# A Fourier mixing layer with a leaky-ReLU MLP: VectorE's work put in the program's own order, with the preparation of the next unit at fixed steps

## The chip, the cores and the metric

The kernel runs on one core of one Trainium2 chip. The time is the device time of one execution in microseconds (us); times given as "the runs" are medians over several executions, and the profile is one further execution, recorded by the hardware profiler. The core has five engines with a queue each: PE (TensorE, the matrix multiplier, whose weight loads are listed apart as PEld), DVE (VectorE), ACT (ScalarE), POOL (GpSimd) and SP (SyncE, which here issues transfers). Each engine works through its own queue in order, and semaphores tie the queues together.

## What is computed

```python
X = np.fft.fft(x, axis=1)            # x: (8, 3008, 256) float32
X = np.fft.fft(X, axis=2)
attn_out = X.real.astype(np.float32)

x = attn_out.reshape(8 * 3008, 256)
h = x @ w_in                          # w_in: (256, 2048)
g = np.maximum(0.01 * h, h)
return (g @ w_out).astype(np.float32) # w_out: (2048, 256)
```

The transform over the 256 features is folded into `w_in` once, at the start; the transform over the 3008 rows is made per batch by folding the rows with additions and subtractions (VectorE) and multiplying the folded rows with small tables of cosines and sines (TensorE).

## The kernel before

**Units, chunks, steps.** Each of the 8 batches is cut into two units by the parity `c` of the output frequency: `units = [(b, c) for b in range(B) for c in (1, 0)]`, so unit number `n` is even for `c = 1` and odd for `c = 0`. A unit has three chunks ("parts" 0, 1, 2) of 250 or 251 columns, and a chunk has 8 steps `f = 0..7`, each of which takes one pair of the 16 blocks of the hidden layer. From chunk 2 on, a step is written (part, f) below; the same (part, f) comes back in every unit, some 16 times in the run.

**What one step does** (`step`, L922). `up` (L818) multiplies a chunk's transformed rows with the folded `w_in` into two PSUM tiles, `cos_ps` and `sin_ps`, by 4 listed matmuls each. `activate` puts them together on VectorE: two scalar_tensor_tensor (L827), one add (L831), one subtract (L832); ScalarE applies the leaky ReLU (L833); GpSimd makes four sums and differences of the result (L840 to L843). `down(at - 3)` multiplies what the step three back made with `w_out` (L891, 14 listed matmuls) into four PSUM tiles `sum_ps`, where all 8 steps of a chunk add up. After a chunk's last step, ScalarE copies one sum (L900), VectorE makes 7 additions out of the four tiles (L915), and SP stores the result. Because of the lag of three steps, those 7 additions stand in step f = 2 of the following chunk. `sum_ps` has four buffers in all, so the first `down` of the following chunk (in step f = 3) writes over the tiles that the 7 additions read. `cos_ps`, `sin_ps` and the transform's `dft_ps` share four other PSUM buffers.

**What is prepared beside it for the next unit.** In an odd unit, `fold_x` folds the rows of the next batch, in eight items: 0 and 2 add the mirrored rows of the first and second half (L327), 1 and 3 fold its columns (L334 and L336), 4 to 7 fold the two halves into each other (L343, one each). `xs[b + 1] = load_x(b + 1)` issues the four transfers of that batch from SP's queue in step (2, 6) of the even unit before; the tile `xt` has one buffer. In every unit but the first and last, `fold_rows` folds the rows further for each of the two feature halves (its `part` 0 and 1) of the next unit: `fold_even` and `fold_odd`, with `turn` (L363 and L364 on ScalarE, L366 and L367 on VectorE) and adds (L393, L394, L402, L403, L406 to L410). `dft` then makes the 16 transform matmuls (L633) and a butterfly of additions on VectorE (L661 to L733), which ends in the tile `mix` that the next unit's `up` reads.

**Who sets the order.** The program is built by a scheduler that orders each engine's queue by its own estimate of when an instruction can start; inside `with tc.manual_schedule(engines={...})` the named engines keep the order in which the program issues their instructions. Before, VectorE has the program's order up to step 34 (the step (1, 2) of unit 1), and from step 35 on the scheduler's. TensorE, ScalarE, GpSimd and SP are ordered by the scheduler from step 16 on, before and after.

Of the kernel before, what the change touches and what calls it, by code (L numbers as in the profile page):

```python
# [271 lines left out]
def tile_fnet_leaky_relu(  # L272
# [35 lines left out]
    def load_x(b):  # L308
        t = x_tile()
        for h in range(2):  # L310
            for odd in range(2):
                load_rows(t, b, h, odd)
        return t
# [10 lines left out]
    def add_mirrors(t, h, rows):  # L324

        a, z = t[:, h, 0, rows], t[:, h, 1, rows]
        nc.vector.tensor_tensor(a, a, z, op=ALU.add)  # L327

    def fold_columns(t, h, part, rows):


        a, z = t[:, h, 0, rows], t[:, h, 1, rows]
        if part == 0:
            nc.vector.tensor_tensor(z[:, :, 0:P], a[:, :, 0:P], a[:, :, P:D], op=ALU.add)  # L334
        else:
            nc.vector.tensor_tensor(z[:, :, P + 1 : D], a[:, :, 1:P], a[:, :, P + 1 : D], op=ALU.subtract)  # L336

    def fold_halves(t, part, c, rows, to=None):

        i, cols = (c + part) % 2, slice(part * P, (part + 1) * P)  # L340
        z = t[:, :, 1, rows, cols]
        to = t[:, i, 0, rows, cols] if to is None else to[:, rows]
        nc.vector.tensor_tensor(to, z[:, 0], z[:, 1], op=(ALU.add, ALU.subtract)[i])  # L343

    def fold_x(b, at):

        t, rows = xs[b], slice(0, NT)
        h, i = divmod(at, 2)
        if h < 2 and i == 0:
            add_mirrors(t, h, rows)  # L350
        elif h < 2:
            for part in range(2):
                fold_columns(t, h, part, rows)
        else:
            fold_halves(t, i, 3 - h, rows)
        if at == 7:
            zs[b] = xs.pop(b)
# [56 lines left out]
    def rows_of_x(b, part, c):  # L414

        t = zs[b]
        src = t[:, (c + part) % 2, 0, :, part * P : (part + 1) * P]
        return Rows(src, [t[:, part, 1].rearrange("p c (i d) -> p (c i) d", i=2)], part, c)

    class Direct:  # L420
# [5 lines left out]
        def even_rows(self, m):  # L426

            pe, n = dft_ps(), (KW[self.c] + 1) // 2
            for i, (chunk, to) in enumerate(((1, pe[0:m, 0 : 2 * n]), (0, pe[0:m, 0:n]), (2, pe[0:m, n : 2 * n]))):
                at, rows = (i + 1) * n if i else 0, slice(0, FROWS if i else P)  # L430
                nc.tensor.matmul(to, lhsT=self.src[rows, chunk], rhs=self.tab[0][rows, at : at + to.shape[1]],  # L431
                                 start=(i == 0), stop=(i == 2), skip_group_check=True)
            return pe

        def odd_rows(self, m, lo=0, hi=KW[1]):

            po, n = dft_ps() if m == P else sum_ps(), KW[1]
            for i in range(FI):
                rows = slice(0, FROWS if i < 2 else P)
                nc.tensor.matmul(po[0:m, 0 : hi - lo], lhsT=self.src[rows, FI + i],  # L440
                                 rhs=self.tab[1 + i // 2][rows, i % 2 * n + lo : i % 2 * n + hi], start=(i == 0), stop=(i == 2))
            return po
# [20 lines left out]

    rows_of = {}

    def fold_rows(u, part):
        rows = rows_of[u, part] = rows_of_x(u[0], part, u[1])
        rows.fold_even()
        rows.fold_odd()


    feat_sb = const.tile([P, 2, 2 * P], F32, name="feat_sb")
# [264 lines left out]
    def mix(u, blk, direct=False):  # L737

        t = work.tile([P, UW[0]], F32, tag=f"mix{blk}", bufs=2, name=f"mix{blk}")
        mixed.setdefault(u, {})[blk] = t  # L740
        return butterfly(t, P, blk, u[1], direct=direct)

    def dft(u, blk):
        rows = rows_of.pop((u, blk))
        banks = even_rows(rows, P), odd_rows(rows, P)
        for made, bank in zip(mix(u, blk), banks):
            made(bank)

    def dft_direct(part):

        rows, made = evens[part], mix(units[1], part, direct=True)
        made[0](rows.even_rows(P))
        po = rows.odd_rows_even(P)
        made[1](po)
        made[2](po)
# [16 lines left out]
    def spread(u):  # L772

        b, c = u
        t = work.tile([P, UW[0]], F32, tag="nb", bufs=2, name="nb")
        nc.sync.dma_start(t[:, 0 : UW[c]], nyq_dram[b, c, 0 : UW[c]].partition_broadcast(P))
        spreads[u] = t
# [18 lines left out]
    units = [(b, c) for b in range(B) for c in PARITIES]  # L796
    blocks, _ = chunks()
    plain = 2
    steps = [(j, f) for f in range(NH) for j in range(plain)]
# [6 lines left out]
    def up(j, f):  # L806
        raised(j, f)
        activate(j, f)
# [108 lines left out]

    lag = 3

    folds = {(0, 1): (0,), (0, 3): (1,), (0, 4): (2,), (0, 5): (3,), (0, 6): (4, 5), (0, 7): (6,), (1, 0): (7,)}  # L920
    first_folds = {(0, 1): (0,), (0, 3): (1,), (0, 4): (2,), (0, 5): (3,), (0, 6): (4,), (0, 7): (5,), (1, 0): (6,), (1, 1): (7,)}

    def step(at):
        if at < len(steps):
            j, f = steps[at]
            up(j, f)
            n, part = divmod(j, 3)
            b, c = units[n]
            if n == 0 and f == 4:
                dft_direct(1)  # L930
            if 0 < n < len(units) - 1:
                if part == 0 and f == 4:
                    spread(units[n + 1])
                at_steps = folds if n > 1 else first_folds
                if n % 2 == 1 and (part, f) in at_steps:
                    for i in at_steps[part, f]:
                        fold_x(b + 1, i)
                if part > 0 and f == 3:
                    fold_rows(units[n + 1], part - 1)
                if part > 0 and f == 5:  # L940
                    dft(units[n + 1], part - 1)
            if n % 2 == 0 and part == 2 and f == 6 and b + 1 < B:
                xs[b + 1] = load_x(b + 1)
        if at - lag >= done:
            down(*steps[at - lag])
# [10 lines left out]
    with tc.manual_schedule(engines={mybir.EngineType.DVE, mybir.EngineType.PE, mybir.EngineType.SP}):  # L956
        with tc.manual_schedule(engines={mybir.EngineType.Pool, mybir.EngineType.Activation}):
# [56 lines left out]
            u, first, others = units[0], (0, CW), (CW, KW[1])  # L1014
# [21 lines left out]
            odd = [direct.odd_rows(P, *first) for direct in (cosine, sine)]  # L1036
# [6 lines left out]
            odd = [direct.odd_rows(P, *others) for direct in (cosine, sine)]  # L1043
# [78 lines left out]
    for at in range(16, 23):  # L1122
        step(at)

    with tc.manual_schedule(engines={mybir.EngineType.DVE}):
        for at in range(23, 35):
            step(at)
    for at in range(35, len(steps) + lag):
        step(at)


# [35 lines left out]
```

## Time and profile before

| what | value |
|---|---|
| median of 4 runs | 1900.11 us (1899.07 to 1901.16) |
| the profiled execution, its own time | 1899.83 us |
| span of its instructions | 1898.0 us |
| granted TensorE clock over the span | 0.999 |
| DVE, L827 (two in a step) | 470 ns each |
| DVE, L831 and L832 | 676 and 669 ns |
| ACT, L833 | 1040 ns |
| POOL, L840 to L843 | 756, 863, 674, 743 ns |
| DVE, L327 / L334 / L336 / L343 (folds of x) | 2139 / 1232 / 1079 / 1288 ns |
| DVE, L366 / L367 (turns) | 617 / 549 ns |
| DVE, L915 (a chunk's last additions) | 408 to 415 ns |
| ACT, L363 / L364 (for the turns) | 391 / 386 ns |

The span is the time from the first to the last instruction that the profiler recorded; the execution's own time is 1.83 us longer. Times inside the trace are counted from the span's start. A row of the trace gives a start, a duration, an engine and a line; a bracket behind it tells how long the engine had been idle and what ended the idle time. Listed durations of neighbouring matmuls overlap, because they are pipelined: what a matmul takes in the stream is the distance between starts, 0.21 us for 250 or 251 columns.

### The profile page before, as it was taken

Reading aid. Unit: us, or ns where it says so; the run is one execution under the profiler, and the core shown is the slowest. Engines: PE = TensorE matmul, PEld = TensorE weight load, DVE = VectorE, ACT = ScalarE, POOL = GpSimd, SP = SyncE. Lnnn points to the kernel's source line nnn. Section 1 sums busy time; section 2 is a strip of 40 time slices with the busy share of each in tenths; the row PEclk is TensorE's granted clock in tenths of the full one; section 3 lists DMA queues with packets and bytes.
Section 4 is the critical chain, followed back from the end, with each engine's and each line's share of the span. In section 5 each row is a group of like instructions: output and inputs, shape, how many; then the busy total and the mean of one; then the engine's idle time right before and its main releaser. Section 6 shows DMA issues by size and latency. Waiting matters only on the chain.

```text
span 1898.0 us, 25260 instructions
## 1 busy us (share of the span) xinstructions
PE 1890.6 (100%) x9088; PEld 1679.7 (89%) x9088; DVE 1275.0 (67%) x2543; ACT 500.8 (26%) x674; POOL 1103.9 (58%) x1510
## 2 busy tenths in 40 slices
PE   9999999999999999999999999999999999999999
PEld 7888888988889888898888988888888888888987
DVE  8857865696656965569555796558865588555554
ACT  3522322232222322223222232222322223222222
POOL 1236555576555765558555675556655566555554
PEclk9999999999999999999999999999999999999999
DMA  7311000110002000020000200002000020000000
GB/s 252 114 62 78 12 20 23 46 74 12 31 11 100 20 22 20 12 108 16 18 20 12 108 22 12 20 12 110 21 12 19 16 115 12 20 12 22 12 12 23
DMA packets 34349, 78.74 MB, mean 41 GB/s; under 512 B 5536, under 2 KB 20000, under 8 KB 34224
## 3 DMA queue, kind: packets, MB, share of 16 engines
q1 hardware_dynamic: 33792, 76.86, 11.0%
q8 instruction: 73, 1.20, 0.3%
q14 instruction: 52, 0.43, 0.1%
q10 hardware_dynamic: 432, 0.26, 0.0%
HBM read 52.40 MB, written 24.71 MB: 41 GB/s over the span
## 4 chain that ended last, share of the span: by engine, by line
PE 98%; DVE 1%; DMA 0%; issue 0%; ACT 0%; DVEq 0%
PE sum_ps L891 58%; PE cos_ps L818 17%; PE sin_ps L818 17%; PE sum_ps L871 3%; PE dft_ps L633 3%; PE wf_ps L577 1%; DMA raw<-in_w_in_dram 0%; DVE xt L327 0%; PE dft_ps L431 0%; DVE xt L334 0%; DVE xt L336 0%; DVE power L542 0%; DVE win L543 0%; DVE power L525 0%; PE dft_ps L458 0%
## 5 line engine op out<-in xcount | busy, mean ns | idle before, releaser
L833 ACT ACTIVATE g<-g 128x1004 f32<-128x1004 f32 (+1 forms) x384 | 399.2, 1040 | 1126.0 <-DVE g L832 1059.5
L827 DVE SCALAR_TENSOR_TENSOR cos<-nb,wn,cos_ps 128x251 f32<-128x251 f32 (+1 forms) x768 | 330.2, 470 | 525.4 <-PE cos_ps L818 523.0
L840 POOL TENSOR_TENSOR s<-g 128x251 f32<-128x251 f32 (+1 forms) x368 | 278.2, 756 | 666.2 <-ACT g L833 660.3
L891 PE MATMUL sum_ps<-s,wt 128*128 128x251 f32 (+1 forms) x2208 | 528.4, 374 | 0.0
L891 PEld LDWEIGHTS sum_ps<-s,wt 128*128 128x128 f32 x2208 | 414.9, 188 | 55.0 <-POOL s L841 1.8
L818 PE MATMUL cos_ps<-mix,wf 128*128 128x251 f32 (+1 forms) x1536 | 387.9, 374 | 0.0
L818 PE MATMUL sin_ps<-mix,wf 128*128 128x251 f32 (+1 forms) x1536 | 387.8, 374 | 0.0
L891 PE MATMUL sum_ps<-g,wo 128*128 128x251 f32 (+1 forms) x1472 | 373.0, 375 | 0.8 <-DVE o L915 0.8
L818 PEld LDWEIGHTS cos_ps<-mix,wf 128*128 128x128 f32 x1536 | 291.2, 190 | 34.2 <-ACT power L526 0.5
L818 PEld LDWEIGHTS sin_ps<-mix,wf 128*128 128x128 f32 x1536 | 290.3, 189 | 34.8
L841 POOL TENSOR_TENSOR s<-s,g 128x251 f32<-128x251 f32 (+1 forms) x368 | 317.7, 863 | 0.0
L891 PEld LDWEIGHTS sum_ps<-g,wo 128*128 128x128 f32 x1472 | 277.0, 190 | 33.0 <-DVE o L915 1.2
L843 POOL TENSOR_TENSOR s<-g,s 128x251 f32<-128x251 f32 (+1 forms) x368 | 273.5, 743 | 28.9
L831 DVE TENSOR_TENSOR g<-cos,sin_ps 128x502 f32<-128x502 f32 (+1 forms) x384 | 259.4, 676 | 43.8 <-DVE cos L827 6.9
L832 DVE TENSOR_TENSOR g<-cos,sin_ps 128x502 f32<-128x502 f32 (+1 forms) x384 | 257.0, 669 | 0.0
L842 POOL TENSOR_TENSOR s<-g 128x251 f32<-128x251 f32 (+1 forms) x368 | 248.2, 674 | 0.0
L891 PE MATMUL sum_ps<-s,wo 128*128 128x251 f32 (+1 forms) x736 | 215.8, 375 | 0.0
L891 PE MATMUL sum_ps<-g,wt 128*128 128x251 f32 (+1 forms) x736 | 215.8, 375 | 0.0
L891 PEld LDWEIGHTS sum_ps<-s,wo 128*128 128x128 f32 x736 | 139.5, 190 | 16.3
L891 PEld LDWEIGHTS sum_ps<-g,wt 128*128 128x128 f32 x736 | 139.8, 190 | 15.8
L915 DVE TENSOR_TENSOR o<-e,sum_ps 128x251 f32<-128x251 f32 (+1 forms) x180 | 66.0, 408 | 0.0
L871 PE MATMUL sum_ps<-g,wo 128*128 128x251 f32 x256 | 57.1, 374 | 0.5 <-DVE wo L543 0.5
(130 smaller groups left out, 825.7 us busy)
## 6 DMA issues: line engine op xcount, KB each, us to landing
xt<-in_x_dram SPq DMA_DIRECT2D x28, 1024.0 KB, 7.6
out_dram<-o SPq DMA_DIRECT2D x78, 251.0 KB, 2.3
raw<-in_w_in_dram SPq DMA_DIRECT2D x8, 512.0 KB, 6.2
raw<-in_w_out_dram SPq DMA_DIRECT2D x8, 512.0 KB, 4.6
out_dram<-o SPq DMA_DIRECT2D x16, 250.0 KB, 2.1
xt<-in_first_x_dram SPq DMA_DIRECT2D x4, 768.0 KB, 8.8
nb<-nyq_dram SPq DMA_DIRECT2D x8, 376.5 KB, 3.4
nb<-nyq_dram SPq DMA_DIRECT2D x7, 376.0 KB, 3.5
```

The lines of the kernel that those rows point to most:

```text
L818: nc.tensor.matmul(pt[blk][:, h * n : (h + 1) * n], lhsT=wf[:, blk, fs[h] * P : (fs[h] + 1) * P], rhs=mixed[b, c][blk][:, at : at + n], st ...
L827: nc.vector.scalar_tensor_tensor(cos[:, hs], in0=spreads[b, c][:, at : at + n], scalar=wn[:, fs[h] : fs[h] + 1], in1=pt[0][:, hs], op0=ALU ...
L831: nc.vector.tensor_tensor(g[:, 0], cos[:, 0 : 2 * n], pt[1][:, 0 : 2 * n], op=ALU.add)
L832: nc.vector.tensor_tensor(g[:, 1], cos[:, 0 : 2 * n], pt[1][:, 0 : 2 * n], op=ALU.subtract)
L833: nc.scalar.activation(g, g, ACT.Lrelu)
L840: nc.gpsimd.tensor_tensor(s1, a[1][0], a[1][1], op=ALU.add)
L841: nc.gpsimd.tensor_tensor(s2, s1, a[0][0], op=ALU.subtract)
L842: nc.gpsimd.tensor_tensor(s3, a[0][0], a[1][0], op=ALU.subtract)
L843: nc.gpsimd.tensor_tensor(s4, a[0][1], s2, op=ALU.subtract)
L871: nc.tensor.matmul(sums[j][d][:, r * n : (r + 1) * n], lhsT=wo[:, fs[h] // NH, fs[h] % NH, d * P : (d + 1) * P], rhs=a[r][h], start=(f == ...
L891: nc.tensor.matmul(sums[j][p], lhsT=still[p], rhs=moving[p], start=(f == 0 and i % 2 == 0), stop=(f == NH - 1), skip_group_check=True)
L915: nc.vector.tensor_tensor(to, x, y, op=ALU.add)
```

## The change

Three things. From step 35 to the end VectorE keeps the program's order, as it did for steps 23 to 34. The eight items of `fold_x` get one list of places for all batches, one item a step, with none at f = 1 or 2 of part 0 (there were two lists, one for the first odd unit and one for the others, and the second put two items in one step). `fold_rows` is split into its even and its odd half, which are issued in successive steps, and the transform of the first feature half is issued two steps later.

| issued in step (part, f) | before, unit 1 | before, later units | after |
|---|---|---|---|
| x items 0 to 7 (odd units) | (0,1) (0,3) (0,4) (0,5) (0,6) (0,7) (1,0) (1,1) | (0,1) (0,3) (0,4) (0,5) (0,6) twice (0,7) (1,0) | (0,3) (0,4) (0,5) (0,6) (0,7) (1,0) (1,1) (1,3) |
| rows, half 0, even / odd | (1,3) / (1,3) | (1,3) / (1,3) | (1,4) / (1,5) |
| transform, half 0 | (1,5) | (1,5) | (1,7) |
| rows, half 1, even / odd | (2,3) / (2,3) | (2,3) / (2,3) | (2,3) / (2,4) |
| transform, half 1 | (2,5) | (2,5) | (2,5) |

```diff
-    def fold_rows(u, part):
-        rows = rows_of[u, part] = rows_of_x(u[0], part, u[1])
-        rows.fold_even()
-        rows.fold_odd()
+    def fold_rows(u, part, odd):
+        if not odd:
+            rows_of[u, part] = rows_of_x(u[0], part, u[1])
+            rows_of[u, part].fold_even()
+        else:
+            rows_of[u, part].fold_odd()
...
-    folds = {(0, 1): (0,), (0, 3): (1,), (0, 4): (2,), (0, 5): (3,), (0, 6): (4, 5), (0, 7): (6,), (1, 0): (7,)}
-    first_folds = {(0, 1): (0,), (0, 3): (1,), (0, 4): (2,), (0, 5): (3,), (0, 6): (4,), (0, 7): (5,), (1, 0): (6,), (1, 1): (7,)}
+    folds = {(0, 3): 0, (0, 4): 1, (0, 5): 2, (0, 6): 3, (0, 7): 4, (1, 0): 5, (1, 1): 6, (1, 3): 7}
+
+    row_folds = {(1, 4): (0, 0), (1, 5): (0, 1), (2, 3): (1, 0), (2, 4): (1, 1)}
+    transforms = {(1, 7): 0, (2, 5): 1}
...
-                at_steps = folds if n > 1 else first_folds
-                if n % 2 == 1 and (part, f) in at_steps:
-                    for i in at_steps[part, f]:
-                        fold_x(b + 1, i)
-                if part > 0 and f == 3:
-                    fold_rows(units[n + 1], part - 1)
-                if part > 0 and f == 5:
-                    dft(units[n + 1], part - 1)
+                if n % 2 == 1 and (part, f) in folds:
+                    fold_x(b + 1, folds[part, f])
+                if (part, f) in row_folds:
+                    fold_rows(units[n + 1], *row_folds[part, f])
+                if (part, f) in transforms:
+                    dft(units[n + 1], transforms[part, f])
...
     with tc.manual_schedule(engines={mybir.EngineType.DVE}):
-        for at in range(23, 35):
+        for at in range(23, len(steps) + lag):
             step(at)
-    for at in range(35, len(steps) + lag):
-        step(at)
```

## The prediction, made before the changed kernel was run

> **What bounds the kernel now.** I read the page's shares and its chain first, then the waits of TensorE, then the timeline around each wait.
>
> ```profile
> PE 1890.6 (100%) x9088; PEld 1679.7 (89%) x9088; DVE 1275.0 (67%) x2543; ACT 500.8 (26%) x674; POOL 1103.9 (58%) x1510
> ...
> PE 98%; DVE 1%; DMA 0%; issue 0%; ACT 0%; DVEq 0%
> ```
>
> TensorE is busy from end to end and is 98% of the chain. The change neither adds nor removes a matmul, so it can only win back moments in which TensorE waits, or make new ones. Its waits from step 23 on, out of the list of waits (us in total, times, longest):
>
> ```profile
> PEld sum_ps L891 <- DVE o L915: 2.3, 7, 1.2
> PEld sum_ps L891 <- POOL s L841: 1.8, 5, 0.4
> ...
> DVE xt L327 <- DMA xt<-in_x_dram: 11.2, 6, 1.9
> ```
>
> To price them I take the distance between the starts of two steps' first `cos_ps` matmuls; I call such a start U. An undisturbed step of 251 columns takes 4.66 to 4.67 us, one with a transform 6.45. After 150 us only six steps are longer. The first is step (1, 3) of unit 1:
>
> ```profile
> 204.67 1.01 PE L818 MATMUL cos_ps<-mix,wf 128*128 128x251 f32 x4
> ...
> 206.87 0.41 DVE L915 TENSOR_TENSOR o<-e,sum_ps 128x251 f32<-128x251 f32 x1
> ...
> 207.33 1.12 PE L891 MATMUL sum_ps<-g,wo 128*128 128x251 f32 x4 [0.80 <-DVE o L915]
> ...
> 210.68 1.01 PE L818 MATMUL cos_ps<-mix,wf 128*128 128x251 f32 x4
> ```
>
> It took 210.68 - 204.67 = 6.01 us, so 1.35 were lost: the first `down` of a new chunk waits until VectorE has read the old sums, and VectorE began that at 206.87, 6.86 after the U of its step (200.01), where an undisturbed chunk begins 3.25 after it (165.96 against 162.71). In front of it stood the row folds that the program issues in step 35, this same (1, 3): the scheduler pulled them forward, and they run from 195.62 on, ahead of the activates of (1, 1) and (1, 2). The other five are steps (0, 3) and look like this, in units 5, 7, 9, 11, 13, 231.17 us apart:
>
> ```profile
> 630.47 1.01 PE L818 MATMUL cos_ps<-mix,wf 128*128 128x251 f32 x4
> 631.59 0.40 DVE L915 TENSOR_TENSOR o<-e,sum_ps 128x250 f32<-128x250 f32 x1
> ...
> 632.62 0.73 DVE L915 TENSOR_TENSOR e<-e,sum_ps 128x250 f32<-128x250 f32 x2
> ...
> 633.14 0.72 PEld L891 LDWEIGHTS sum_ps<-s,wt 128*128 128x128 f32 x4 [0.35 <-POOL s L841]
> ```
>
> The next U is 635.43, so 4.96 us, 0.30 lost. The row names GpSimd, but the L841 that this `down` needs had ended at 629.40; what ended at about 633.0 is the third addition, which frees the second sum tile. It is the same wait. VectorE was late because the scheduler had put the first fold of x as early as the load allowed (it began at 612.39 after 1.84 us of waiting for the transfer) and the following folds between the halves of activates.
>
> So what is to be won: 1.35 + 5 x 0.30 = 2.85 us. The margin of an undisturbed step: the third addition ends at U + 4.4 and is needed at U + 4.66 + 1.69 + 0.85 = U + 7.2 (next step, its 8 `up` matmuls, 4 of `down`). VectorE may thus be some 2.8 us late at a chunk's end, and in other steps more: in unit 5 the activates of three steps in a row began 4.6 to 4.95 after U instead of 1.05, and no step was longer.
>
> **The change, part by part.**
>
> *Folds of x.* The same 10 instructions per batch: 2 x 2.14 (L327) + 2 x (1.23 + 1.08) + 4 x 1.29 = 14.1 us of VectorE, now one item a step at (0,3) to (1,0), (1,1), (1,3). A step has 4.66; an activate takes 2.17 (its first L827 to the next free slot); 2.49 are left, and no item is longer than 2.14 to 2.46. The source order with almost this list has already run, in unit 1:
>
> ```profile
> 173.08 0.86 DVE L827 SCALAR_TENSOR_TENSOR cos<-nb,wn,cos_ps 128x251 f32<-128x251 f32 x2
> ...
> 175.26 2.49 DVE L327 TENSOR_TENSOR xt<-xt 128x2048 f32<-128x2048 f32 x1
> 177.74 0.86 DVE L827 SCALAR_TENSOR_TENSOR cos<-nb,wn,cos_ps 128x251 f32<-128x251 f32 x2
> ...
> 180.27 1.22 DVE L334 TENSOR_TENSOR xt<-xt 128x1024 f32<-128x1024 f32 x1
> 181.41 1.21 DVE L336 TENSOR_TENSOR xt<-xt 128x1016 f32<-128x1016 f32 x1
> 182.53 0.86 DVE L827 SCALAR_TENSOR_TENSOR cos<-nb,wn,cos_ps 128x251 f32<-128x251 f32 x2
> ```
>
> With U at 172.03, 176.69 and 181.35 these activates start 1.05, 1.05 and 1.18 after U: VectorE is full but never behind, and the steps are 4.66. Cost 0. The wait for the load (11.2 us in six) goes: item 0 comes after the activate of (0, 3), in unit 5 at about 630.47 + 3.31 = 633.8, against 612.39; the load stays in step (2, 6). What hides the folds is VectorE's free 2.5 us a step; in the worst of these rows an item of 2.83 (L327 at 612.39) puts the next activate 3.31 + 2.83 - 5.71 = 0.43 later, far under the margin.
>
> *No fold at a chunk's end.* Step (0, 2) keeps 2.17 + 7 additions. In source order they end before or at the next activate's due time U + 5.71 (U = 162.71: additions 165.96 to 168.54, next activate 168.45, 0.04 late). Step (1, 1) has an item of 1.29: 3.31 + 1.29 = 4.6 < 5.71, so (1, 2) starts on time. Behind the additions, which wait for ScalarE's copy and the last `down`, only the next activate is queued. So all six late chunk ends go: -2.85. Bounds: 0, if another instruction takes the same place, and -2.85, for there is no other wait to win.
>
> *Rows, split.* No instruction more. Even half: two turns, 0.62 + 0.55 = 1.17, or in even units L393 + L394 = 0.63. Odd half for `c = 1`: 4 turns 2.33 + L402 and L403 0.85 = 3.2; for `c = 0` 0.42 + 0.59 + 0.68 + 0.76 + 1.17 = 3.6. After an activate that ends at U + 3.31 this ends at U + 6.5 or 6.9, and the next activate is up to 1.2 late, then on time again. For half 0 two steps follow before the transform. For half 1 the odd fold is in (2, 4) and the transform in (2, 5): its first 8 matmuls start at U + 4.66 + 1.69 (602.49 - 600.80) and its odd ones about 0.9 later, at U + 7.25. Margin 0.35 to 0.75 us. The near row costs 0. The far one: every turn 0.88 (L367 at 644.17) with ScalarE's four copies behind its activation (4.47 + 4 x 0.39 = 6.03, then two turns 1.76 and two adds 0.82) ends at U + 8.6, a loss of 1.35 in each of the seven odd units, +9.5. I take 0: in this trace ScalarE makes its copies ahead (four of them at 195.78, before the folds that read them), and VectorE's turns run in 0.34 (420.27) when GpSimd is idle, which it is up to U + 4.54.
>
> *Transform of half 0 two steps later.* 16 matmuls in either place; its butterfly is 3.5 to 4.3 us in a step of 6.45 (2.17 + 4.3 = 6.5, nothing late by over a us), the next chunk end is three steps off, and `mix` is needed eight steps later. No transfer moves: the load, the spreads and the stores keep their steps on SP. Cost 0.
>
> *GpSimd beside the folds.* L843 takes 1.74 us beside L334 (at 624.68) and 0.72 without it; in unit 1's fold steps its last result still came at most 8.6 after U, against 7.3, and is needed over 15 after. Cost 0. [...]
>
> **Sum.** 1898.0 - 2.85 = 1895.15 span, + 1.83 = 1896.98 against the profiled execution's 1899.83. The median of the runs is 0.28 above that execution: 1897.3.
>
> **Rivals.**
> 1. *The late chunk ends stay, or as much is lost elsewhere* (the scheduler's estimate moves other queues): 1899 to 1900.1. For it: TensorE's, ScalarE's and GpSimd's order is still the scheduler's. Against: TensorE's order is the source's throughout this trace.
> 2. *The odd row fold becomes the wait*: the transform of (2, 5) waits for VectorE. Price 0 to 1.35 in seven units, up to 1897.3 + 9.5 = 1906.8; it makes the kernel slower than before from 2.85 / 7 = 0.41 each, and measurably so from (2.85 + 3.8) / 7 = 0.95. For it: the margin of 0.35. Against: ScalarE's lead.
> 3. *More is won than the six waits*: over 3.8, so 1896.3 or less. For it nothing but spread: steps are as long beside folds (4.66) as in quiet units (4.67 from 235.80 to 240.47), so matmuls are not slowed by VectorE.
>
> **Chances.** A measurement of this kernel tells 0.2%, 3.8 us, from no change. Forecast (six waits go) 0.72; rival 1 0.10; rival 2 0.10, of which 0.06 is slower by over 0.2%; rival 3 0.08, to which the forecast's lower spread adds 0.04. Faster 0.12, same 0.82, slower 0.06. The likeliest case alone spans 1896.2 to 1898.4 (0.28 for the profiled run against the median, and 0.8 for another set of runs); to hold rival 1 the range goes to 1900.2, and down to 1896.0.
>
> **What would show it.** Right: no step of 6.01 or 4.96 left, no wait of L891 for L915 or L841 over 0.1 us, no wait of L327 for a transfer, activates at most 1.5 late. Wrong: L633 waiting for L402, L403 or L410 in steps of over 6.46; or L915 starting over 5 after its step's U.

## The result, and the profile after

| | before | after |
|---|---|---|
| median of the runs | 1900.43 us (60 runs, 1898.36 to 1904.0) | 1898.04 us (42 runs, 1896.44 to 1901.0) |
| ratio, 95% interval | | 0.9986 (0.9982 to 0.9990) |
| profiled execution, its own time / span | 1899.83 / 1898.0 us | 1898.86 / 1897.0 us |
| start of step 24 (its U) | 153.41 us | 155.24 us |
| from there to the end of the last matmul | 1739.92 us | 1737.09 us |

The ratio is a gain of 1900.43 x 0.0014 = 2.7 us (1.9 to 3.4 by the interval), less than the 0.2% that was named as the limit between a change and none. The forecast was 2.85 us and 1897.3 us.

The two profiled spans differ by 1.0 us only, and the last two rows of the table say why: from step 24 on, where the six late chunk ends lie, 2.83 us were won, and in this one execution the start-up came out 1.83 us longer. The start-up's instructions are the same in both kernels.

The page of the kernel after, its busy times and the engines' shares of the chain of waits:

```profile
PE 1889.3 (100%) x9088; PEld 1682.0 (89%) x9088; DVE 1267.3 (67%) x2543; ACT 500.9 (26%) x674; POOL 1055.9 (56%) x1510
...
PE 99%; DVE 0%; DMA 0%; ACT 0%; issue 0%; SPq 0%; DVEq 0%; POOL 0%; POOLq 0%
```

The chain has lost its 1% of VectorE. VectorE's busy time fell by 7.7 us and GpSimd's by 48, with the same instructions: they were longer before because more of them ran beside each other. The sums that GpSimd makes in L843 (L841 before) show it; their mean came down from 863 to 739 ns. From 150 us on, 85 of them before ran beside a VectorE instruction whose inputs all lie in SBUF and took 1.35 us on average, and the 276 others took 0.72; after, 42 ran so, at 0.90, and 320 took 0.72. None of that is on the path.

The waits of TensorE's matmuls in the kernel after, all of them (us in total, times, longest):

```profile
PE sum_ps L873 <- ACT g L835: 1.4, 1, 1.4
PE sum_ps L956 <- POOL blank L961: 1.1, 1, 1.1
PE sum_ps L873 <- DVE wo L545: 0.5, 1, 0.5
```

All three lie in the start-up. No wait of L893 (the `down`, L891 before) is left, among the weight loads neither, and the 11.2 us in which L327 waited for its transfer are gone: the list has no such line any more. (Lines of the kernel after are 2 higher than before, those above 465.)

The timeline of unit 5 after, steps (0, 2) and (0, 3); the second was 4.96 us long before:

```profile
626.29 1.01 PE L820 MATMUL cos_ps<-mix,wf 128*128 128x251 f32 x4
...
629.52 0.41 DVE L917 TENSOR_TENSOR o<-e,sum_ps 128x250 f32<-128x250 f32 x1
629.88 1.26 DVE L917 TENSOR_TENSOR e<-e,sum_ps 128x250 f32<-128x250 f32 x3
...
630.94 1.01 PE L820 MATMUL cos_ps<-mix,wf 128*128 128x251 f32 x4
...
634.20 2.29 DVE L327 TENSOR_TENSOR xt<-xt 128x2048 f32<-128x2048 f32 x1
...
635.60 1.01 PE L820 MATMUL cos_ps<-mix,wf 128*128 128x251 f32 x4
```

The additions begin 629.52 - 626.29 = 3.23 after their step's U, and the fold of x that had delayed them now starts behind the activate of (0, 3), at 634.20 (worked out before: 633.8). The step is 635.60 - 630.94 = 4.66 us. No step after 150 us is longer than its kind in a quiet unit.

### The profile page after: what moved, and what is told of

Same layout as the page of the kernel before. It is cut to its first block, busy times and chain, and to the rows that moved or that the text cites. A ratio compares the mean times of both kernels' runs of the same rounds, so it can differ in the third digit from the quotient of the medians.

```text
span 1897.0 us, 25288 instructions
## 1 busy us (share of the span) xinstructions
PE 1889.3 (100%) x9088; PEld 1682.0 (89%) x9088; DVE 1267.3 (67%) x2543; ACT 500.9 (26%) x674; POOL 1055.9 (56%) x1510
## 4 chain that ended last, share of the span: by engine, by line
PE 99%; DVE 0%; DMA 0%; ACT 0%; issue 0%; SPq 0%; DVEq 0%; POOL 0%; POOLq 0%
PE sum_ps L893 58%; PE sin_ps L820 17%; PE cos_ps L820 17%; PE sum_ps L873 3%; PE dft_ps L635 3%; PE wf_ps L579 1%; PE sum_ps L956 1%; PE dft_ps L431 0%; DMA wn<-wf 0%; PE dft_ps L440 0%; PE sum_ps L440 0%; DVE cos L829 0%; DVE g L833 0%; PE dft_ps L458 0%; PE dft_ps L453 0%
## 5 line engine op out<-in xcount | busy, mean ns | idle before, releaser
L835 ACT ACTIVATE g<-g 128x1004 f32<-128x1004 f32 (+1 forms) x384 | 399.3, 1040 | 1136.6 <-DVE g L834 1116.3
L842 POOL TENSOR_TENSOR s<-g 128x251 f32<-128x251 f32 (+1 forms) x368 | 280.5, 762 | 711.3 <-ACT g L835 705.4
L893 PE MATMUL sum_ps<-s,wt 128*128 128x251 f32 (+1 forms) x2208 | 527.6, 374 | 0.0
L893 PEld LDWEIGHTS sum_ps<-s,wt 128*128 128x128 f32 x2208 | 415.9, 188 | 52.4
L893 PE MATMUL sum_ps<-g,wo 128*128 128x251 f32 (+1 forms) x1472 | 372.8, 375 | 0.0
L893 PEld LDWEIGHTS sum_ps<-g,wo 128*128 128x128 f32 x1472 | 277.4, 190 | 31.6
L845 POOL TENSOR_TENSOR s<-g,s 128x251 f32<-128x251 f32 (+1 forms) x368 | 259.4, 705 | 28.9
L843 POOL TENSOR_TENSOR s<-s,g 128x251 f32<-128x251 f32 (+1 forms) x368 | 272.0, 739 | 0.0
L844 POOL TENSOR_TENSOR s<-g 128x251 f32<-128x251 f32 (+1 forms) x368 | 256.2, 696 | 0.0
L893 PE MATMUL sum_ps<-g,wt 128*128 128x251 f32 (+1 forms) x736 | 215.8, 375 | 0.0
L893 PE MATMUL sum_ps<-s,wo 128*128 128x251 f32 (+1 forms) x736 | 215.8, 375 | 0.0
L893 PEld LDWEIGHTS sum_ps<-s,wo 128*128 128x128 f32 x736 | 139.5, 190 | 16.3
L893 PEld LDWEIGHTS sum_ps<-g,wt 128*128 128x128 f32 x736 | 139.8, 190 | 15.9
L917 DVE TENSOR_TENSOR o<-e,sum_ps 128x251 f32<-128x251 f32 (+1 forms) x180 | 66.0, 409 | 0.0
L873 PE MATMUL sum_ps<-g,wo 128*128 128x251 f32 x256 | 57.2, 375 | 1.9 <-ACT g L835 1.4
```

The source lines that it names most:

```text
L835: nc.scalar.activation(g, g, ACT.Lrelu)
L842: nc.gpsimd.tensor_tensor(s1, a[1][0], a[1][1], op=ALU.add)
L843: nc.gpsimd.tensor_tensor(s2, s1, a[0][0], op=ALU.subtract)
L844: nc.gpsimd.tensor_tensor(s3, a[0][0], a[1][0], op=ALU.subtract)
L845: nc.gpsimd.tensor_tensor(s4, a[0][1], s2, op=ALU.subtract)
L873: nc.tensor.matmul(sums[j][d][:, r * n : (r + 1) * n], lhsT=wo[:, fs[h] // NH, fs[h] % NH, d * P : (d + 1) * P], rhs=a[r][h], start=(f == ...
```

## The experiments

All times are medians; "lost" is the stretch from step 24's U to the end of the last matmul against the 1737.09 us of the kernel after. That stretch is the sharper measure: it leaves out the start-up, which varies by itself.

| kernel | median | ratio to before (95%) | the stretch | lost |
|---|---|---|---|---|
| before | 1900.43 | | 1739.92 | 2.83 |
| after | 1898.04 | 0.9986 (0.9982 to 0.9990) | 1737.09 | 0 |
| order_only | 1898.22 | 0.9989 (0.9980 to 0.9998) | 1737.09 | 0 |
| places_only | 1900.59 | 1.0002 (0.9993 to 1.0011) | 1740.11 | 3.02 |
| order_unit1 | 1898.89 | 0.9995 (0.9986 to 1.0003) | 1738.01 | 0.92 |
| one_at_end | 1897.59 | 0.9987 (0.9978 to 0.9995) | 1737.09 | 0 |
| two_at_end | 1905.33 | 1.0031 (1.0020 to 1.0043) | 1745.31 | 8.22 |
| two_at_end_pe | 1929.32 | 1.0156 (1.0142 to 1.0170) | 1768.99 | 31.90 |
| odd_late | 1901.9 | 1.0010 (1.0001 to 1.0020) | 1741.72 | 4.63 |

Ratios are against runs of the kernel before on the same chip.

**order_only: the order without the places.** The kernel before, with its old lists of places, and VectorE in the program's order to the end.

```diff
     with tc.manual_schedule(engines={mybir.EngineType.DVE}):
-        for at in range(23, 35):
+        for at in range(23, len(steps) + lag):
             step(at)
-    for at in range(35, len(steps) + lag):
-        step(at)
```

> The places of before (x items at f = 1 of part 0 and two in (0, 6), rows whole at f = 3, transforms at f = 5), but VectorE in the program's order to the end. Theory A (the order wins, the places do not matter): no step longer than 4.68 or 6.46, all six waits gone, 2.85 less than before, about 1897.6 against 1900.4 (ratio 0.9985); item 0 in (0, 1) ends at 3.3 + 2.1 = 5.4 after its U, before the next activate is due. Theory B (the places are needed too): late chunk ends at (0, 3) as before, 5 x 0.30 or more still lost, 1899.1 or above.

Its VectorE in unit 5, out of the timeline; the U of step (0, 2) is 625.74:

```profile
624.32 2.28 DVE L327 TENSOR_TENSOR xt<-xt 128x2048 f32<-128x2048 f32 x1
626.79 0.86 DVE L827 SCALAR_TENSOR_TENSOR cos<-nb,wn,cos_ps 128x251 f32<-128x251 f32 x2 [0.19 <-PE cos_ps L818]
...
628.97 0.41 DVE L915 TENSOR_TENSOR o<-e,sum_ps 128x250 f32<-128x250 f32 x1
```

The fold stands one step ahead of the chunk's end, as the old list has it, and the additions begin at U + 3.23 all the same. The stretch is that of the kernel after to the hundredth. So the program's order on VectorE is enough for the whole gain, with the old places.

**places_only: the places without the order.** The kernel after, with VectorE left to the scheduler from step 35 on, as before.

```diff
-        for at in range(23, len(steps) + lag):
+        for at in range(23, 35):
             step(at)
+    for at in range(35, len(steps) + lag):
+        step(at)
```

> The new places, but VectorE from step 35 on in the scheduler's order, as before. Theory A: the scheduler pulls the folds forward to where the load allows whatever step issues them, so the five steps of 4.96 stay and L327 still waits for its transfer: 1.5 to 2.9 of the loss remain, 1899 to 1900.4 (ratio 0.999 to 1.000). Theory B: the places alone do it, 1897.6.

Its list of waits, and below it unit 1 at step (1, 3) out of the timeline:

```profile
PEld sum_ps L893 <- DVE o L917: 2.6, 6, 1.7
...
DVE xt L327 <- DMA xt<-in_x_dram: 11.2, 6, 2.0
```

```profile
207.53 1.01 PE L820 MATMUL cos_ps<-mix,wf 128*128 128x251 f32 x4
...
208.78 0.34 DVE L366 SCALAR_TENSOR_TENSOR xt<-xt,angle 95x128 f32<-95x128 f32 x1
...
210.22 0.40 DVE L917 TENSOR_TENSOR o<-e,sum_ps 128x251 f32<-128x251 f32 x1
...
210.67 1.11 PE L893 MATMUL sum_ps<-g,wo 128*128 128x251 f32 x4 [1.28 <-DVE o L917]
...
214.01 1.01 PE L820 MATMUL cos_ps<-mix,wf 128*128 128x251 f32 x4
```

The row folds are issued in (1, 4) here, two steps after the one with the chunk's last additions, and the scheduler still put them in front of these additions: the turn at 208.78 runs ahead of the L917 at 210.22, and the step is 214.01 - 207.53 = 6.48, 0.47 longer than before. The fold of x still waits for its transfer, six times, although it is issued two steps later. So the scheduler put the folds far ahead of the place where the program issues them, in both kernels. How far is seen in the additions L393 and L394 for `c = 0`, which the program first issues in unit 2, in the kernel before at (1, 3), whose U is 321.55: it ran the first of them at 196.66, in unit 1. They stand among the rows from 195.62 on that the prediction put down to step 35 alone; in order_only the first runs at 324.74.

**order_unit1: the order for unit 1 only.** The kernel before, in the program's order to step 47.

```diff
-        for at in range(23, 35):
+        for at in range(23, 48):
             step(at)
-    for at in range(35, len(steps) + lag):
+    for at in range(48, len(steps) + lag):
         step(at)
```

> The kernel before, with the program's order kept 13 steps longer, to step 47, the end of unit 1. Theory A: only the wait of 6.01 - 4.66 = 1.35 in step (1, 3) of unit 1 goes, the five steps of 4.96 stay: 1899.1 (ratio 0.9993). Theory B (the waits hang together, or each has another cause): the 1.35 stays or turns up later, 1900.4.

The step of unit 1 is 4.66 again. Of the five steps of 4.96 only three are there (units 5, 7 and 11), so 0.92 were lost where five would lose 1.5. In units 9 and 13 VectorE's order is the same, but the third addition ended 6.55 and 6.50 after U instead of 7.2. The difference goes back to L327, which started as soon as its transfer had landed: at U - 13.52 and U - 13.62 in these two, and at U - 13.46 to U - 13.37 in the three that lost. In the kernel before, unit 3 is the like: its third addition ended at U + 6.55, and nothing was lost.

What a tenth of a microsecond in a landing changes is whether L327 or one of GpSimd's sums, L842 (L844 in places_only), starts first. In the kernel before, unit 3 (nothing lost) and unit 5 (0.30 lost), out of the timeline:

```profile
381.44 2.29 DVE L327 TENSOR_TENSOR xt<-xt 128x2048 f32<-128x2048 f32 x1 [1.76 <-DMA xt<-in_x_dram]
381.49 2.81 POOL L842 TENSOR_TENSOR s<-g 128x250 f32<-128x250 f32 x1
...
612.36 0.71 POOL L842 TENSOR_TENSOR s<-g 128x250 f32<-128x250 f32 x1
612.39 2.83 DVE L327 TENSOR_TENSOR xt<-xt 128x2048 f32<-128x2048 f32 x1 [1.84 <-DMA xt<-in_x_dram]
```

In both pairs the one that starts second is held up for most of the other's time: the sum takes 2.81 instead of 0.64, its mean where nothing runs beside it, and the fold 2.83 instead of 2.29. The three kernels in which this fold waits for its transfer (before, places_only, order_unit1) have 18 such places: in 6 the fold came first, by 0.003 to 0.156 us, took 2.29 to 2.35 and nothing was lost; in 12 the sum came first, by 0.002 to 0.141 us, the fold took 2.72 to 2.86, and each of these lost 0.30.

**one_at_end and two_at_end: how much a chunk's end bears.** The kernel after, with one fold of x (2.28 us) or a fold and its columns in (0, 2), in front of the chunk's last additions. The row folds stay as they are after the change. The two lists, one a kernel:

```diff
-    folds = {(0, 3): 0, (0, 4): 1, (0, 5): 2, (0, 6): 3, (0, 7): 4, (1, 0): 5, (1, 1): 6, (1, 3): 7}
+    folds = {(0, 2): (0,), (0, 3): (1,), (0, 4): (2,), (0, 5): (3,), (0, 6): (4,), (0, 7): (5,), (1, 0): (6,), (1, 1): (7,)}
...
+    folds = {(0, 2): (0, 1), (0, 4): (2,), (0, 5): (3,), (0, 6): (4,), (0, 7): (5,), (1, 0): (6,), (1, 1): (7,)}
...
-                    fold_x(b + 1, folds[part, f])
+                    for i in folds[part, f]:
+                        fold_x(b + 1, i)
```

> The changed kernel with x item 0 (L327, 2.14 to 2.5) in (0, 2), ahead of the chunk's seven additions, and the others one step earlier each. Theory A (a chunk end has a margin of 2.8): the first addition starts at about U + 5.5 to 5.8, the third ends at 6.7 to 7.0, needed at 7.2: no step longer, 1897.6 as the changed kernel. Theory B (any fold at a chunk end costs): 0.3 or more in each of seven odd units, 1899.7 or above.

> The changed kernel with x items 0 and 1 (4.6 together) in (0, 2), ahead of the additions; the scheduler, which sees them late in its own estimate, puts the `down` of (0, 3) behind the `up` of (0, 4) on TensorE. Theory A: first addition at U + 7.9, and TensorE comes to it 1.69 later than before, so 0.3 to 1.3 are lost in each of seven odd units: 1899.7 to 1906.7. Theory B (the margin is not what limits): no loss, 1897.6.

VectorE and TensorE of one_at_end in unit 5, out of the timeline:

```profile
625.30 1.01 PE L820 MATMUL cos_ps<-mix,wf 128*128 128x251 f32 x4
...
628.52 2.28 DVE L327 TENSOR_TENSOR xt<-xt 128x2048 f32<-128x2048 f32 x1
630.73 0.41 DVE L917 TENSOR_TENSOR o<-e,sum_ps 128x250 f32<-128x250 f32 x1
631.05 1.19 DVE L917 TENSOR_TENSOR e<-e,sum_ps 128x250 f32<-128x250 f32 x3
...
631.64 1.01 PE L893 MATMUL sum_ps<-g,wo 128*128 128x251 f32 x4
```

The additions begin 2.2 us late, at U + 5.43, and the first `down` into the freed tile starts at 631.64 without a wait. One fold at a chunk's end therefore costs nothing, seven times over.

In two_at_end the additions begin at U + 8.65, and it costs 8.22 / 7 = 1.17 us a unit. TensorE's own wait at such a place:

```profile
403.25 0.40 DVE L917 TENSOR_TENSOR o<-e,sum_ps 128x250 f32<-128x250 f32 x1
...
403.71 1.54 PE L893 MATMUL sum_ps<-g,wo 128*128 128x251 f32 x6 [0.91 <-DVE o L917]
```

The time lies in what was expected, and it is not the price of the lateness alone, for TensorE's order changed too: the scheduler put the `up` of (0, 4) ahead of the `down` of (0, 3), 8 matmuls or 1.7 us of cover. A further kernel takes that cover away.

**two_at_end_pe: the same with TensorE held in the program's order.**

```diff
-    with tc.manual_schedule(engines={mybir.EngineType.DVE}):
+    with tc.manual_schedule(engines={mybir.EngineType.DVE, mybir.EngineType.PE}):
```

> As the run with two items at the chunk end, with TensorE in the program's order too, so that `down` stays ahead of the next `up`. Theory A (margin 2.8): the first sum tile is free at U + 8.3 and wanted at U + 6.35, so about 2.0 are lost in each of seven odd units, 14 in all: 1911.6 (ratio 1.0059), in steps (0, 3) of about 6.6. Theory B: no loss or one of a whole fold, 4.6 x 7 = 32.

The wait was the expected one, and its price was missed by more than half: 31.9 us lost, 4.56 in each of seven steps. That this is close to theory B's 32, the price of a whole fold, is chance, as the two terms below show. The timeline of unit 3, where U of (0, 2) is 399.18:

```profile
402.40 2.28 DVE L327 TENSOR_TENSOR xt<-xt 128x2048 f32<-128x2048 f32 x1
...
404.72 1.62 DVE L334 TENSOR_TENSOR xt<-xt 128x1024 f32<-128x1024 f32 x1
...
406.26 1.64 DVE L336 TENSOR_TENSOR xt<-xt 128x1016 f32<-128x1016 f32 x1
...
407.82 0.40 DVE L917 TENSOR_TENSOR o<-e,sum_ps 128x250 f32<-128x250 f32 x1
...
408.28 1.74 PE L893 MATMUL sum_ps<-g,wo 128*128 128x251 f32 x4 [2.60 <-DVE o L917]
...
409.81 2.54 PE L893 MATMUL sum_ps<-s,wt 128*128 128x251 f32 x6
```

Two things differ. The column folds took 1.62 and 1.64 us instead of 1.23 and 1.08, the means of the table before, which hold shorter ones of the start-up too; in unit 1 before they took 1.22 and 1.21. Here GpSimd ran beside them all the time (busy for 4.45 of the 4.45 us from 403.83 to 408.28); GpSimd's own sums, 0.63 to 0.72 alone, took 1.54 to 1.68 there. And the matmuls behind the wait were slow: six in 2.54 us, where six take 1.44. The windows of that stretch (the first number is the length of the window; PEclk is the granted clock):

```profile
core 0: us, PE busy (x) PEld busy (x) DVE busy (x) ACT busy (x) POOL busy (x), PEclk, DMA share, GB/s
...
408.28:408.60 0.32, 0.32 (x2) 0.30 (x3) 0.28 (x2) 0.00 (x0) 0.24 (x2) 1.00 0.00 0
408.60:412.02 3.42, 3.42 (x10) 2.77 (x9) 3.29 (x9) 0.00 (x0) 0.68 (x1) 0.50 0.35 135
412.02:413.03 1.01, 1.01 (x6) 0.91 (x5) 0.45 (x1) 0.44 (x1) 0.00 (x0) 0.99 0.14 52
```

For 3.42 us after the wait the clock was 0.50. The two terms add up: the matmul before the wait started at 405.31 and the one behind it at 408.28, 2.97 apart instead of 0.21, so 2.76 were idle; 3.42 us at half speed lose another 1.71; together 4.47 of the 4.56.

**odd_late: the odd row fold beside its transform.** The kernel after, with the odd half of feature half 1 issued in (2, 5), the step of its transform.

```diff
-    row_folds = {(1, 4): (0, 0), (1, 5): (0, 1), (2, 3): (1, 0), (2, 4): (1, 1)}
+    row_folds = {(1, 4): (0, 0), (1, 5): (0, 1), (2, 3): (1, 0), (2, 5): (1, 1)}
```

> The changed kernel with the odd row fold of half 1 in (2, 5), ahead of the transform that reads it: the second rival of the prediction, made sure. The scheduler puts `down` ahead of the odd transform on TensorE where its estimate has the rows late. Theory A (the odd fold then sets the end): it ends at U + 3.3 + 2.4 = 5.7 for c = 1 and about 6.3 for c = 0; TensorE comes to the odd rows at U + 5.55 and to the last of them at about U + 5.3: 0.1 to 1.0 lost in each of 14 units, 1 to 14 in all, 1899 to 1911. Theory B (TensorE's changed order hides it): 1897.6.

It lost 4.63. TensorE in step (2, 5) of unit 2, out of the timeline:

```profile
369.43 1.01 PE L820 MATMUL cos_ps<-mix,wf 128*128 128x250 f32 x4
...
375.50 0.46 PE L635 MATMUL dft_ps<-tab,xt 95*128 95x95 f32 x2 [0.15 <-DVE xt L367]
376.25 1.01 PE L820 MATMUL cos_ps<-mix,wf 128*128 128x250 f32 x4
```

The step is 6.82 us where the kernel after has 6.43, in seven units; in the other seven it is 6.70 against 6.45. Together 7 x 0.39 + 7 x 0.25 = 4.5. So the wait that rival 2 feared exists: the change's place, (2, 4), is the last one that costs nothing. The price stayed small because TensorE filled most of the lateness: the even transform matmuls do not need the odd fold, and in all 14 units the scheduler put matmuls of a `down` ahead of the odd ones, all 14 in the odd units and 10 in the even ones.

## Why the prediction was right, step by step

**What was to be won** came out as said: the six waits went, and nothing took their place, 2.83 us against 2.85 from step 24 on. The median moved by 2.4 and the ratio by 2.7 (1.9 to 3.4), an interval that holds the 2.83. If the runs do gain a little less than the trace, it fits the 0.30 of steps (0, 3): under the scheduler's order three of the five came in order_unit1 and four in places_only, so not every run of the kernel before need lose all five. That is argued from these two, not counted in the runs. The predicted time is 0.74 too low: 0.32 of it is the level (the 60 runs of the kernel before have a median of 1900.43, the four shown had 1900.11), the rest this smaller gain.

**No fold at a chunk's end** was the right amount in the sum, under a name that credits the wrong part. The step let order and places act together; order_only and places_only tell them apart, and the places are worth nothing here: with the old ones the order wins all, and without the order the new ones win nothing. one_at_end says it from the other side: even a fold just ahead of the additions is free.

**The margin of 2.8 us** at a chunk's end was put a little too high. Third additions that ended at U + 6.50 to 6.63 lost nothing, those at U + 7.20 lost 0.30. So the margin over the normal U + 4.45 lies between 2.2 and 2.75. The prediction took the start of the matmul as the time at which the tile is needed; what waits is its weight load, one matmul earlier. In unit 5 after, where nothing waits and the U of step (0, 2) is 626.29:

```profile
633.28 1.25 PEld L893 LDWEIGHTS sum_ps<-s,wt 128*128 128x128 f32 x6
633.49 1.44 PE L893 MATMUL sum_ps<-s,wt 128*128 128x251 f32 x6
```

The load starts at U + 6.99. Where it waits, it starts 0.12 after the addition's end (633.14 in the prediction's rows of unit 5, where the addition begun at 632.62 ends at 633.02), so the third addition may end at U + 6.87: a margin of 2.4. In the kernel before the chunk ends stood on both sides of this edge, which is why single ones of the 0.30 come and go.

**Folds of x**, cost 0: right, with two sizes too small. The latest activate starts 1.81 after its U, in (0, 7) of unit 5, so it is 0.76 late where 0.43 was the worst worked out; the limit named was 1.5. In front of it the two column folds took 1.64 and 1.72 us, and not the 1.23 and 1.08 of the sum. It costs nothing. The wait for the load is gone.

**Rows, split**, cost 0: right, and with more room than was worked out. The odd half of `c = 1` in the kernel after, on VectorE, in step (2, 4), whose U is 712.01:

```profile
715.24 0.34 DVE L366 SCALAR_TENSOR_TENSOR xt<-xt,angle 95x128 f32<-95x128 f32 x1
...
716.75 0.93 DVE L403 TENSOR_TENSOR xt<-xt 95x256 f32<-95x256 f32 x1
717.73 0.86 DVE L829 SCALAR_TENSOR_TENSOR cos<-nb,wn,cos_ps 128x251 f32<-128x251 f32 x2
```

It took 717.68 - 715.24 = 2.4 us instead of 3.2. The means of the trace before had the turns at 0.55 to 0.62 because 70 of the 112 ran beside GpSimd, at 0.73 on average, and the 42 others took 0.34; here they take 0.34, as the one row at 420.27 had said. It ends at 717.68 - 712.01 = U + 5.67, so the margin is 7.25 - 5.67 = 1.6, not 0.75. The 0.35 was the margin for `c = 0`; there the odd half ends at U + 6.02 instead of 6.9, in all seven units, and leaves 1.2. odd_late shows what would have come had the step been missed.

**Transform two steps later**, cost 0: right; no step is over 6.46.

**GpSimd beside the folds**, cost 0: right. Its last result came at most 8.5 us after U in the fold steps, against 7.3 in quiet ones and up to 8.4 in the steps with a transform. Over the five steps (0, 3) to (0, 7) of unit 5 it stood at 8.17, 8.36, 8.48, 8.52 and 8.06: later by 0.85 in the first and by 1.2 in the fourth. That the two engines hold each other up is seen in the rows of L327 and L842 above and in two_at_end_pe (0.7 against 1.6 us); here GpSimd is back at 7.34 in (1, 0), the next fold step.

**The rivals.** 1 fell: no late end stayed. 2 fell for the place that the change chose, and odd_late shows its mechanism. 3 fell: what was won is not over the six waits.

## What to carry to other kernels

If a scheduler's estimate puts work that nobody waits for (folds for a later unit) ahead of the reads that free an accumulator, move the order, not the places: hold that one engine in the program's order and try it alone first. Measure the slack at such a place by putting a known instruction there on purpose; here 2.2 us of it were free, and with TensorE's order held 5.4 us cost 4.56. And compare kernels over the stretch that they differ in: the start-up moved by as much as the whole gain.

## What the runs showed of the hardware

**Behind a wait of 2.6 us TensorE's clock was 0.50 for 3.42 us.** two_at_end_pe has seven waits of 2.60 us (18.2 in all), one in each of the seven odd units with folds of x. In unit 3 the wait ended at 408.28, and the clock was 0.50 from 408.60 to 412.02; it was 1.00 from 399.18 to 408.60, the wait included, 0.99 from 412.02 to 413.03 and 1.00 from there to 418.00. In unit 5 the six matmuls behind the wait took 2.64 us, as slow as the 2.54 in unit 3. The mean clock of the profiled execution was 0.994, which is what seven such stretches make of a clock of 1.00: 1 - 7 x 3.42 x 0.50 / 1928.4 = 0.994. Behind the waits of 0.91 (two_at_end) and 1.28 (places_only) the clock stayed at 1.00 (403.70 to 408.00 and 207.00 to 216.00), and the mean of two_at_end, which has seven of the first kind, was 1.000. What a wait between 1.28 and 2.60 us does was not measured.

**The start-up varies by some 3 us.** Over the nine profiles U of step 24 is 153.2 to 156.3, with one order of instructions. It goes with one wait of TensorE, that of the L873 shown above for ScalarE's L835: no such wait at 153.2 and 153.4, 0.7 at 154.0 and 154.25, 0.8 at 154.1, 1.0 at 154.4, 1.2 at 154.7, 1.4 at 155.2 and 2.5 (in two) at 156.3. Ahead of it VectorE waits for the small transfers of `wn`; in the kernel after, out of its list of waits:

```profile
DVE cos L829 <- DMA wn<-wf: 4.6, 3, 2.1
```

In the kernel before it was one wait of 1.3, the earliest of these places, and TensorE did not wait. In the seven profiles with a wait of TensorE there, VectorE's wait for `wn` some 3 us ahead of it is longer by 0.66 to 0.70 each time (2.07 and 1.41 in the kernel after, 1.37 and 0.70 in odd_late). That the landing of these transfers sets the start-up is read from these nine profiles; that it makes the spread of the runs (1896.44 to 1901.0) is argued, and neither was tried by itself.
